# PV as register-addressed TensorE loops in a written order: one decode step over a long KV cache

## The chip, the cores and the metric

One core of one Trainium2 chip. The metric is the device time of one execution in microseconds (us). All executions quoted here were fast (none was over 1.5% above the fastest of the same kernel), and each changed kernel is compared with runs of the kernel before on the same chip. Ratios are the mean time of one kernel's fast runs over that of the other's of the same rounds, so not quite the ratio of the medians that stand beside them.

## The reference

One token through an adaLN-conditioned block: modulation, layer norm, grouped-query attention over a cache of 32768 positions, then a ReLU feed-forward part. All tensors are bf16.

```python
# D = 512, Hq = 32, Hkv = 8 (4 q heads to a kv head), Sk = 32768, Dh = 128, Dff = 1792
sa, ca, ga, sb, cb, gb = split(silu(c) @ w_mod, 6)
h = layernorm(x) * (1 + ca) + sa
q = h @ wq
p = softmax(q @ k_cache.T * Dh ** -0.5)       # per kv head: 4 x 32768
x = x + ga * ((p @ v_cache) @ wo)
h = layernorm(x) * (1 + cb) + sb
out = x + gb * (relu(h @ w1) @ w2)
```

K and V are 134 MB of the 149 MB that the kernel reads.

## The kernel before

The loads run on one queue through a ring of four slots of 4 MB; a load can be issued only when the tile that held its slot has been used for the last time. For each kv head g, a K half is transposed by VectorE and multiplied with a block-diagonal q (`scores`), the softmax follows, and PV (probabilities times V) multiplies 16 columns of the transposed probabilities by V, 64 matmuls a head, accumulated in one bank `o_ps`. While head g's PV runs, head g+1's scores are taken. Cut to what the change and the argument touch:

```python
ring = ctx.enter_context(tc.tile_pool(name="ring", bufs=4))
...
stream = [("wm",), ("wq",)] + [("k", 0, (2 * G, 2 * G + 1)) for G in range(NG)]
for g in range(LAST):
    for G in range(NG):
        stream += [(kind, gg, (2 * G, 2 * G + 1)) for kind, gg in (("k", g + 1), ("v", g))]
stream += [("v", LAST, (0, 1)), ("v", LAST, (2,)), ("wo", 0), ("wo", 1), ("v", LAST, (3,)), ("wo", 2)]
stream += [("w1",)] + [("w2", i) for i in range(len(W2P))]
...
def pv(g, u, js=range(16)):
    ...
    Vsb = need(("v", g, u))
    if g == LAST and u > 1:                       # the narrow form: V as weights
        for j in range(TK):
            nc.tensor.matmul(oT_ps, lhsT=Vsb[:, j, :], rhs=PT_g[:, j % 16, c0:c0 + REP], ...)
        return
    ...
    for j in js:                                  # the wide form
        m = nc.tensor.matmul(
            o_tiles[g][:], lhsT=PT_g[:, j, REP * s0:REP * (s0 + 4)],
            rhs=Vsb.rearrange("p (s j) d -> p s j d", j=16)[:, :, j, :],
            start=(u == 0 and j == 0), stop=(u == end and j == 15))
        pe_order(m)
    if u == end and j == 15:                      # diagonal blocks of o_ps, summed by TensorE
        X = spool.tile([16, 4 * Dh], F32, tag="X", name="X", bufs=1)
        nc.scalar.copy(out=X[:], in_=o_tiles.pop(g)[:])
        for s in range(4):
            nc.tensor.matmul(oT_ps, lhsT=X[:, s * Dh:(s + 1) * Dh], rhs=osel[:, s, :], ...)
...
for g in range(Hkv):                              # order of the program; a scheduler moves within it
    if g + 1 < Hkv:
        build_qbd(g + 1)
    for G in range(NG):
        for u in (2 * G, 2 * G + 1):
            if g + 1 < Hkv:
                scores(g + 1, u)
        if g + 1 < Hkv and G == NG - 1:
            stages = softmax(g + 1)
            pv(g, 2 * G, range(8));  next(stages)
            pv(g, 2 * G, range(8, 16));  next(stages)
            pv(g, 2 * G + 1);  next(stages, None)
            continue
        for u in (2 * G, 2 * G + 1):
            if g == LAST and u == NTILE - 1:
                for i in range(len(WOP) - 1):
                    project(i)
                join_rows()
            pv(g, u)
    normalise(g)
    ...
project(len(WOP) - 1)
```

## Time and profile before

| | before |
|---|---|
| median of 4 runs | 357.38 us (356.87 to 357.7) |
| span of the profiled run | 356.0 us |
| bytes on the load queue | 149.43 MB, 98.0% of the span |
| TensorE, VectorE busy | 81%, 54% |

The prediction below shows the rows that matter most: DMA full to the last slice, K and V landing 29 us after their issue.

This is how TensorE enters the end, from its timeline (start, length, engine, line, operation, output and inputs, count, and the idle time before with what ended it):

```profile
323.59 1.05 PE L468 MATMUL acc_ps<-osel,X 16*128 16x4 f32 x8 [0.35 <-ACT X L466]
324.57 7.07 PE L458 MATMUL o_ps<-Vsb,PT_g 128*16 128x512 bf16 x32
333.35 1.84 PE L448 MATMUL acc_ps<-PT_g,Vsb 128*128 128x4 bf16 x64
```

The last head's PV starts at 324.57 us.

### The profile page before, as it was taken

What the parts mean: (1) busy time and instruction counts of PE and PEld (TensorE: products, weight loads), DVE (VectorE), ACT (ScalarE), POOL (GpSimd) and SP (SyncE); (2) the same over time, 40 slices, a digit from 0 to 9 for tenths busy, and PEclk for the clock granted to TensorE, in tenths of its full rate; (3) what the DMA queues carried; (4) which work ended last, traced back from release to release, by engine and by line L of the source; (5) the groups of instructions that cost most, each with busy time, mean ns of one, the idle gap of its engine ahead of it and who ended that gap; (6) DMA issues with size and microseconds to landing.
All of it is one profiled execution on the core that took longest, in us unless ns stands there. A gap on an engine that the chain in (4) does not pass through costs nothing.

```text
span 356.0 us, 3635 instructions
## 1 busy us (share of the span) xinstructions
PE 287.1 (81%) x1571; PEld 128.5 (36%) x1571; DVE 191.6 (54%) x219; ACT 34.0 (10%) x78; POOL 8.5 (2%) x14
## 2 busy tenths in 40 slices
PE   0466965999699969788896969896978879799874
PEld 0253322444334433334332334333333424244473
DVE  8524697782667366463819373746637290842020
ACT  1023003102100110012000200012000200011020
POOL 9000000000000000000000000000000000000000
PEclk9966789999879998999899969999899969899755
DMA  8999999999999999999999999999999999999993
GB/s 326 437 435 436 423 443 427 422 446 427 429 438 435 420 447 431 423 442 429 431 438 427 433 439 423 438 436 423 435 442 419 442 431 422 442 427 419 390 407 138
DMA packets 6602, 149.66 MB, mean 420 GB/s; under 512 B 697, under 2 KB 698, under 8 KB 1594
## 3 DMA queue, kind: packets, MB, share of 16 engines
q1 hardware_dynamic: 6578, 149.43, 98.0%
q8 instruction: 12, 0.20, 0.2%
q14 instruction: 4, 0.03, 0.0%
q10 hardware_dynamic: 8, 0.00, 0.0%
HBM read 149.42 MB, written 0.00 MB: 420 GB/s over the span
## 4 chain that ended last, share of the span: by engine, by line
DMA 55%; PE 22%; DVE 16%; issue 4%; ACT 1%; SPq 0%; DVEq 0%; ACTq 0%
DMA Ksb<-in_A_k_cache_dram 50%; DVE KTt L375 14%; PE S_ps L384 9%; PE o_ps L458 6%; DMA c_row<-in_c_dram 3%; DMA w_sb<-in_B_w_dram 2%; PE modT_ps L284 1%; PE acc_ps L448 1%; PE q_ps L267 1%; PE mod_ps L267 1%; PE a_ps L510 1%; PE qT_ps L334 1%; PE acc_ps L468 1%; PE acc_ps L530 1%; ACT L243 0%
## 5 line engine op out<-in xcount | busy, mean ns | idle before, releaser
L384 PE MATMUL S_ps<-KTt,qbd 128*128 128x512 bf16 x512 | 135.6, 423 | 39.1 <-DVE KTt L375 39.1
L375 DVE STREAM_TRANSPOSE KTt<-Ksb 128x2048 f32<-128x2048 f32 x64 | 142.5, 2280 | 34.4 <-DMA Ksb<-in_A_k_cache_dram 32.8
L458 PE MATMUL o_ps<-Vsb,PT_g 128*16 128x512 bf16 x480 | 108.4, 379 | 0.0
L384 PEld LDWEIGHTS <-qbd 128*128 128x128 bf16 x512 | 53.4, 105 | 114.8 <-issue 64.4
L458 PEld LDWEIGHTS <-PT_g 128*16 128x16 bf16 x480 | 40.8, 90 | 60.0 <-issue 6.0
L390 DVE TENSOR_SCALAR_CACHE_REDUCE S_g<-S_ps 128x512 f32<-128x512 f32 x16 | 11.1, 692 | 37.7 <-PE S_ps L384 37.7
L355 ACT COPY qbd<-qrep_sb 32x128 bf16<-32x128 bf16 x32 | 9.4, 295 | 161.5 <-PE S_ps L384 160.4
L427 DVE STREAM_TRANSPOSE PT_g<-P_g 128x1024 bf16<-128x1024 bf16 x8 | 9.9, 1238 | 21.7 <-ACT P_g L422 21.7
L482 DVE TENSOR_TENSOR oT_sb<-acc_ps,Linv 128x4 bf16<-128x4 f32 x8 | 1.3, 162 | 25.7 <-PE acc_ps L448 17.2
L468 PE MATMUL acc_ps<-osel,X 16*128 16x4 f32 x64 | 8.4, 250 | 3.2 <-ACT X L466 3.2
L419 ACT ACTIVATE nbias<-Mb_ps 128x1 f32<-128x1 f32 x8 | 1.4, 171 | 89.1 <-PE Mb_ps L417 89.1
L203 PE MATMUL xc_ps<-one,c_bd 8*128 8x1 bf16 x4 | 0.3, 171 | 11.8 <-DVE c_bd L193 11.8
L468 PEld LDWEIGHTS acc_ps<-osel,X 16*128 16x128 f32 x64 | 7.7, 186 | 4.3 <-ACT X L466 4.3
L422 ACT ACTIVATE P_g<-S_g,nbias 128x1024 bf16<-128x1024 f32 x8 | 9.2, 1149 | 0.4 <-ACT nbias L419 0.2
L155 DVE COPY sel<-ident_bf 128x128 bf16<-128x128 bf16 x4 | 7.2, 3544 | 0.0
L466 ACT COPY X<-o_ps 16x512 f32<-16x512 f32 x8 | 4.6, 574 | 22.8 <-PE o_ps L458 22.8
L406 DVE TENSOR_REDUCE Mrow<-mT_ps 1x4 f32<-1x128 f32 x8 | 2.2, 278 | 8.2 <-PE mT_ps L404 8.2
L267 PE MATMUL q_ps<-wq_sb,hT 128*1 128x512 bf16 x32 | 3.6, 627 | 2.6 <-DVE hT L250 2.6
L435 DVE RECIPROCAL Linv<-L_ps 128x4 f32<-128x4 f32 x8 | 1.4, 176 | 7.0 <-PE L_ps L433 7.0
L417 PEld LDWEIGHTS Mb_ps<-ident_f,Mexp 1*128 1x128 f32 x16 | 2.3, 182 | 6.1 <-issue 6.1
L203 PEld LDWEIGHTS <-c_bd 8*128 8x128 bf16 x4 | 0.2, 112 | 11.8 <-DVE c_bd L193 11.8
L284 PE MATMUL modT_ps<-rowsel,mod_rows 128*128 128x4 f32 x16 | 3.9, 375 | 0.5 <-ACT mod_rows L279 0.5
(112 smaller groups left out, 96.6 us busy)
## 6 DMA issues: line engine op xcount, KB each, us to landing
Ksb<-in_A_k_cache_dram SPq DMA_DIRECT2D x16, 4096.0 KB, 29.7
Vsb<-in_A_v_cache_dram SPq DMA_DIRECT2D x15, 4096.0 KB, 28.9
wq_sb<-in_A_wq_dram SPq DMA_DIRECT2D x1, 4096.0 KB, 18.8
Vsb<-in_A_v_cache_dram SPq DMA_DIRECT2D x2, 2048.0 KB, 16.3
wm_sb<-in_w_mod_dram SPq DMA_DIRECT2D x1, 3072.0 KB, 10.3
wo_sb<-in_A_wo_dram SPq DMA_DIRECT2D x1, 2048.0 KB
wo_sb<-in_A_wo_dram SPq DMA_DIRECT2D x2, 1024.0 KB, 9.9
w_sb<-in_B_w_dram SPq DMA_DIRECT2D x1, 1792.0 KB, 9.9
```

The lines of the kernel that those rows point to most:

```text
L155: nc.vector.tensor_copy(out=sel[:, hp, :].rearrange("p (a c) -> p a c", a=4), in_=src)
L267: nc.tensor.matmul(dst[j // 4][32 * (j % 4):32 * (j % 4) + 1, :], lhsT=src_T[:, kt:kt + 1], rhs=w[:, kt, j * 512:(j + 1) * 512], start=(kt ...
L284: nc.tensor.matmul(modT_ps[:, i, ko, :], lhsT=mod_rows[:, i, :].rearrange("q (m ko) -> q ko m", ko=KT)[:, ko, :], rhs=rowsel[:], start=Tru ...
L355: nc.scalar.copy(out=o, in_=i)
L375: nc.vector.transpose(out=KTt[:].bitcast(F32), in_=Ksb[:, 32 * half:32 * half + 32, :].rearrange("p j d -> p (j d)").bitcast(F32),)
L384: nc.tensor.matmul(S_ps, lhsT=qbd[g % 2][:, hp, s, :], rhs=KTv[:, 16 * sl:16 * sl + 16, h, :, par], start=(t4 == 0 and sl == 0 and hp == 0 ...
L390: nc.vector.tensor_scalar(out=S_tiles[g][:, G, :], in0=S_ps, scalar1=1.0, scalar2=None, op0=ALU.mult, op1=ALU.max, accum_out=m_tiles[g][:, ...
L422: nc.scalar.activation(out=P_g[:], in_=S_g[:].rearrange("p g f -> p (g f)"), func=ACT.Exp, bias=nbias[:], scale=scale, accum_out=l_g[:],)
L427: nc.vector.transpose(out=PT_g[:], in_=P_g[:])
L458: m = nc.tensor.matmul(o_tiles[g][:], lhsT=PT_g[:, j, REP * s0:REP * (s0 + 4)], rhs=Vsb.rearrange("p (s j) d -> p s j d", j=16)[:, :, j, : ...
L466: nc.scalar.copy(out=X[:], in_=o_tiles.pop(g)[:])
L468: nc.tensor.matmul(oT_ps, lhsT=X[:, s * Dh:(s + 1) * Dh], rhs=osel[:, s, :], start=(s == 0), stop=(g < LAST and s == 3), skip_group_check= ...
```

## The change

The intent: a shorter TensorE program (PV of six of the eight kv heads as loops over byte offsets), TensorE and VectorE in a written order instead of the scheduler's, the softmax's steps taken between score steps, the masked sum of the four diagonal blocks on VectorE in four steps, and a front with fewer small matmuls. Cut to its core (the front, the renamed tiles and the split of `wo` into 2+4+2 heads, of which the first two parts share a slot, are left out):

```diff
+    LOOPED = Hkv - 2
-    def pv(g, u, js=range(16)):
+    def pv(g, us, js=range(16)):
...
+        if g < LOOPED:
+            with tc.tile_critical():
+                with nc.tensor.Fori(0, 512 - 63, 64) as at:
+                    for b in range(2):
+                        for u, V in zip(us, Vf):
+                            step(u, V, PTf[:, 32 * b + 16 * (u % 2):][:, bass.DynSlice(at, 16)],
+                                 V[:, :, Dh * b:][:, :, bass.DynSlice(at * (Dh // 32), Dh)])
+        else:
+            for u, V in zip(us, Vf):
+                for j in js: ...
-            nc.scalar.copy(out=X[:], in_=o_tiles.pop(g)[:])
-            for s in range(4):
-                nc.tensor.matmul(oT_ps, lhsT=X[:, s * Dh:(s + 1) * Dh], rhs=osel[:, s, :], ...)
+    def blocks(g):
+        nc.vector.tensor_scalar(out=Y[:], in0=o[:, 0], scalar1=smask[:, 0:1], ...)
+        for s in range(1, 4):
+            nc.vector.scalar_tensor_tensor(out=Y[:], in0=o[:, s], scalar=smask[:, s:s + 1], in1=Y[:], ...)
+        if g == LAST:
+            nc.vector.memset(oT_ps, 0.0)
+    def o_cols(g):
+        nc.tensor.matmul(oT_ps, lhsT=Y_tiles.pop(g)[:], rhs=qsel, ...)
+    with tc.manual_schedule(engines={mybir.EngineType.PE, mybir.EngineType.DVE}):
+        ...
+        for g in range(LAST):
+            h = g + 1
+            build_qbd(h)
+            turn_k(h, 0, 0)
+            if soft: next(soft)          # Mrow, Mexp on VectorE: wait for mT on TensorE
+            scores(h, 0, 0)
+            if soft: next(soft)          # Mb, exp
+            open_o(g)                    # VectorE fills o_ps with zeros
+            turn_k(h, 0, 1); scores(h, 0, 1)
+            if g > 0: blocks(g - 1); o_cols(g - 1)
+            turn_k(h, 1, 0); scores(h, 1, 0); turn_k(h, 1, 1); scores(h, 1, 1)
+            ...                          # PT transpose, normalise(g - 1), L, bank_max(h, 0), Linv
+            pv(g, (0, 1))
+            for u in (2, 3): ...         # turn_k, scores
+            bank_max(h, 1)
+            soft = softmax(h)
+            next(soft)                   # m_p
+            if g < LOOPED:
+                pv(g, (2, 3))
+                next(soft)               # mT on TensorE, behind the loop
+                continue
+            next(soft); next(soft)
+            pv(g, (2,), range(6)); ...; pv(g, (2,), range(6, 16)); pv(g, (3,)); ...
+            open_o(LAST); blocks(g); o_cols(g); normalise(g)
+        pv(LAST, (0, 1)); pv(LAST, (2,))
+        blocks(LAST); project(0); o_cols(LAST); project(1); join_rows()
+        pv(LAST, (3,)); normalise(LAST)
+    project(len(WOP) - 1)
```

## The prediction

> **What bounds the kernel now.** I read the page's time slices and queue table first, then the chain that ended last, then the SyncE queue's own waits, then the timeline of one kv head, then the end.
>
> ```profile
> PE   0466965999699969788896969896978879799874
> DMA  8999999999999999999999999999999999999993
> GB/s 326 437 435 436 423 443 427 422 446 427 429 438 435 420 447 431 423 442 429 431 438 427 433 439 423 438 436 423 435 442 419 442 431 422 442 427 419 390 407 138
> q1 hardware_dynamic: 6578, 149.43, 98.0%
> DMA 55%; PE 22%; DVE 16%; issue 4%; ACT 1%; SPq 0%; DVEq 0%; ACTq 0%
> ```
>
> The DMA row is full from the first slice to the last but one. Slices 2 to 36 average 432.5 GB/s, and 149.43 MB at that rate are 345.5 us of the 356.0. The other 10.5 us are the start (slice 1 moves 326 GB/s, some 2.2 us lost), the smaller rows of the last weights (390 and 407 GB/s), and some 5 us after the last bytes. So compute matters only where it lets the queue run dry, or after the last byte. Does it run dry?
>
> ```profile
> SPq L118 <- DVE KTt L375: 134.3, 15, 12.4
> SPq L118 <- PE o_ps L458: 72.3, 8, 9.9
> SPq L118 <- PE L_ps L433: 66.3, 7, 10.5
> Ksb<-in_A_k_cache_dram SPq DMA_DIRECT2D x16, 4096.0 KB, 29.7
> Vsb<-in_A_v_cache_dram SPq DMA_DIRECT2D x15, 4096.0 KB, 28.9
> ```
>
> SyncE waits for ring slots (four of 4 MB), but a 4 MB load lasts 9.7 us at that rate and lands 29 us after its issue: on average two loads are still ahead of it. These waits are slack, not loss.
>
> ```profile
> 129.65 8.88 DVE L375 STREAM_TRANSPOSE KTt<-Ksb 128x2048 f32<-128x2048 f32 x4
> 140.71 7.07 PE L458 MATMUL o_ps<-Vsb,PT_g 128*16 128x512 bf16 x32
> 147.58 8.89 DVE L375 STREAM_TRANSPOSE KTt<-Ksb 128x2048 f32<-128x2048 f32 x4 [6.06 <-DMA Ksb<-in_A_k_cache_dram]
> 152.14 1.90 PE L384 MATMUL S_ps<-KTt,qbd 128*128 128x512 bf16 x8 [0.30 <-DVE KTt L375]
> 350.22 1.02 PE L601 MATMUL ffn_ps<-w_sb,hidT 128*1 128x128 bf16 x32 [1.59 <-DMA w_sb<-in_B_w_dram]
> 351.50 1.02 PE L601 MATMUL ffn_ps<-w_sb,hidT 128*1 128x128 bf16 x24 [0.26 <-DMA w_sb<-in_B_w_dram]
> ```
>
> A head's four loads take 38.7 us (K transposes at 108.85 and again at 147.58 in the full timeline). In them TensorE has four blocks of 32 matmuls at 221 ns (7.07 us), two for scores and two for PV, 28.3 us, and about 1.8 us of small ones: some 8 us of slack per head. VectorE sits idle until a K load lands. The last FFN matmuls wait for the weights' arrival, and from the last arrival (352.10) to the end are 3.9 us. The kernel is bound by its loads.
>
> [...] In this trace 64 pairs of weight load and matmul of the o_T step take 1.84 us, 29 ns a pair[...]. [...] The instruction queue here moved 0.20 MB, 0.2% of the engines' span, so the shorter program (2759 listed TensorE rows become 2072) can save a tenth of a microsecond or so.
>
> **The change, part by part.** Bytes, load order (but for the two first parts of wo, swapped in size) and slots stay. So each part is counted against slack first.
>
> *Front.* Sixteen modT matmuls (3.90 us) become eight fp32 transposes; one such took 0.27 us (the mT row), so 2.2 us. Thirty-two gb matmuls (1.16 us) become one of about 0.5. The q path from 28.85 to 31.94 (copies, 16 matmuls of 2.14 us, a cast) becomes two VectorE transposes of 512 columns (2280 ns for 2048 columns, so about 0.6 us each) and small copies, about 1.7 us. Sum: some 3.5 us earlier, but the first K load lands only at about 30 us[...], so the first transpose moves from 32.4 to about 30. Nothing of this reaches the queue, which then has 10 us and more ahead. Worth 0.
>
> *PV as loops.* Twelve loops of 8 turns with 4 matmuls. Each matmul has one fused register instruction[...] before it, each turn an add and a compare-and-branch. [...] So 8 to 10 us, with 9 as the centre, where it was 7.07.
>
> *A wait that the diff doesn't show.* In the built program the branch into each loop waits for every semaphore at its value in the program so far. One is the K load behind the V that the loop needs, so PV of V(g,01) starts only when K(g+1,23) has landed, 9.7 us later than it might. V's slot comes free later by that much. With K(h,01) landing at 0, V at 9.7, K(h,23) at 19.4: PV loop of the head before 0 to 9, max, scores with softmax and the masked sum between, paced by three transposes in turn behind Mrow, up to 20.4; loop to 29.4, scores and bank maximum to 37.4; next K at 38.7. So a period is 19.4 + 2 x loop, in 38.7: it fits up to a loop of 9.65 us. V's slot is free at 29.4 and its next load must be issued by about 36.7 (the load ahead ends at 38.7): 7 us to spare. The queue stays fed.
>
> *Written order, masked sum.* The X copy (0.57 us on ScalarE) and 8 acc matmuls (1.05 us, 0.7 us of wait in front) become four VectorE sums[...] beside transposes and one matmul: about 1 us less of TensorE per head, in slack.
>
> *End.* PV of V(7,2) is 16 wide matmuls (3.5 us) for 64 narrow ones (1.84), and TensorE comes some 4 us later into the end, held back by the late K wait. But v7(3) is now issued after PV of head 6, not after that of v7(0,1), and w1 after v7(2): one step sooner each. My reckoning leaves the stream 1 to 2 us of slack there. After the last weights the chain is the same: 3.9 us.
>
> Sum: 0 from the front, 0 from the middle, between -0.5 and +1 at the end: **357.5 us**.
>
> **The rivals.** *TensorE becomes the bound.* If a loop costs more than 9.65 us, each head lags by twice the excess; 11 us would be 2.7 us a head, 15 us over five and a half heads, of which some slack is there first: 365 to 370 us. For it: nobody has measured register-addressed matmuls here, and TensorE is already 81% busy. Against: [...]a lag of up to 7 us in V's slots starves nothing. *The late K wait becomes the bound.* With slots freed 9.7 us later, any further stall[...] would let the queue run dry in every head: 360 to 368. For it: the written order makes VectorE's Mrow wait for TensorE's mT behind the loop, and the first half of a head already needs 20.4 of 19.4 us in my sum. Against: the second half gives back 2. *Faster.* If the dips at the end (390 and 407 GB/s) came from late issues, the earlier issues would return up to 2 us: 355.5. Against: in the trace those loads were issued before the stream reached them. Under 350.2 (2% faster) it cannot come: 345.5 us of transfers, 2 at the start and 4 after the last arrival are 351.5.
>
> **Range and chances.** The centre is the bound of the loads, which doesn't move. Up to 1.5 us below it lies the best end; above, half of the two slower rivals. A loop over 10.4 us (over 2% in all) gets 0.17. Range 355.5 to 365; faster 0.02, same 0.80, slower 0.18.
>
> **What would show each step.** The DMA row full to the last slice but one and GB/s near 432 in the middle: bound unchanged. A loop's 32 matmuls in 7 to 9.5 us; over 9.7 with TensorE at 95% and GB/s falling is the first rival. PV's first matmul just after the landing of the next K load, and V's time from issue to landing fallen from 28.9 to about 20 us (K's to 21 to 25): the late wait. First K transpose near 30 us. The last weights landing 3.9 us before the end. The prediction is wrong if the GB/s slices of the middle fall below 425, or if the last weights land over 2 us sooner or later than 352.

The loop's sum (register instructions, weight loads and matmuls, add and branch, the way in and out) came to 8 to 10 us a loop, with 9 as the centre; it is the author's estimate and no more. It enters the forecast as nothing, since 9 is under the 9.65 us that fit: 357.5 us is the time before, 357.38 us, with 0 from the front, 0 from the middle and -0.5 to +1 us at the end. Two smaller terms are cut too: what made up the landing of the first K load at about 30 us, and the length of one of VectorE's four sums (measured later: 293 ns for the first, 339 ns for each of the others).

## More of the kernel before

One more view is needed for the end. These are windows of 4 us; the columns are the length, the busy time of TensorE's matmuls, of its weight loads, of VectorE, ScalarE and GpSimd, then TensorE's granted clock as a share of full speed, the DMA share and GB/s.

```profile
336.00:340.00 4.00, 3.31 (x27) 1.80 (x19) 0.00 (x0) 1.87 (x2) 0.00 (x0) 0.50 0.93 387
340.00:344.00 4.00, 3.23 (x92) 3.08 (x93) 0.56 (x3) 0.00 (x0) 0.00 (x0) 0.50 1.05 448
344.00:348.00 4.00, 3.13 (x86) 2.85 (x84) 1.48 (x11) 0.56 (x2) 0.00 (x0) 0.50 0.95 366
348.00:352.00 4.00, 2.16 (x72) 1.85 (x70) 0.00 (x0) 0.18 (x1) 0.00 (x0) 0.50 0.59 223
```

The loads keep up their rate to about 348 us.

## The result, and the profile after

The changed kernel took 368.98 us (median of 4 runs, 366.08 to 369.79) beside 357.38 us for the kernel before: ratio 1.0311, 95% interval 1.025 to 1.0373. It is slower, and outside the predicted range. The rows of the page after that answer to those of before:

```profile
DMA  8999999999999999999999999999999999996572
GB/s 329 438 428 442 419 439 431 431 442 424 436 428 435 442 424 436 428 431 445 420 442 428 429 442 425 443 419 435 438 428 445 417 436 438 420 426 292 169 286 63
q1 hardware_dynamic: 6592, 149.43, 95.2%
PE 14%; DVE 4%; issue 0%; ACT 0%; DVEq 0%
L490 PE MATMUL o_ps<-Vsb,PT_g 128*16 (+1 forms) x496 | 128.0, 401 | 21.3 <-ACT qbd L387 7.6
Vsb<-in_A_v_cache_dram SPq DMA_DIRECT2D x15, 4096.0 KB, 17.3
```

Slices 2 to 36 average 432.3 GB/s, as before. The middle of the kernel lost nothing. The four last slices hold the whole loss, and the chain that ended last, which was 55% DMA before, now has no DMA in it as far as it could be followed: the end waits for TensorE and VectorE. The windows of the end, as shown for before and with the one ahead:

```profile
332.00:336.00 4.00, 3.29 (x9) 1.42 (x10) 1.01 (x4) 0.00 (x0) 0.00 (x0) 0.55 1.03 434
336.00:340.00 4.00, 4.00 (x12) 1.34 (x11) 0.00 (x0) 0.00 (x0) 0.00 (x0) 0.60 0.36 152
340.00:344.00 4.00, 4.00 (x20) 1.69 (x19) 0.00 (x0) 0.00 (x0) 0.00 (x0) 1.00 0.00 0
344.00:348.00 4.00, 2.68 (x13) 1.00 (x12) 1.18 (x4) 0.00 (x0) 0.00 (x0) 1.00 0.93 305
348.00:352.00 4.00, 2.90 (x26) 0.95 (x25) 0.87 (x4) 0.22 (x1) 0.00 (x0) 0.68 0.84 337
```

The queue runs dry from about 338 to 344 us and then is fed in pieces. TensorE's timeline says why:

```profile
332.71 0.58 PE L528 MATMUL acc_ps<-mask_sb,Y 16*128 16x4 f32 x2 [2.16 <-DVE Y L520]
333.23 13.45 PE L490 MATMUL o_ps<-Vsb,PT_g 128*16 128x512 bf16 x48
348.83 0.60 PE L572 MATMUL a_ps<-wo_sb,o_sb 128*1 128x512 bf16 x8 [2.15 <-DVE a_ps L243]
```

The last head's PV starts at 333.23 us where it was 324.57: 8.66 us later, of which 2.16 are a wait for VectorE's four sums (before, the wait at this place was 0.35 us). Its 48 matmuls take 13.45 us. At the full clock they take 10.53 (experiment e5 has them so). The clock fell to about half behind the wait: the window from 332 to 336 us has 0.55. The kernel before also ran at 0.50 from 336 us on, without such a wait, so the wait is not the only way into the half clock. PV frees the slots: the last part of wo was issued at 343.26 us (before: 335.22), w1 at 346.71 (337.04). Nothing was issued for 13 us before that.

Why is TensorE late? One head of the timeline, all engines but the weight loads, with cuts:

```profile
151.34 8.04 PE L490 MATMUL o_ps<-Vsb,PT_g 128*16 x32 [0.80 <-DVE Linv L471]
159.57 7.10 PE L419 MATMUL S_ps<-KTt,qbd 128*128 128x512 bf16 x32 [0.19 <-PEq L496]
...
166.70 1.22 ACT L387 COPY qbd<-qrep_sb 32x128 bf16<-32x128 bf16 x4 [24.09 <-PE S_ps L419]
...
168.56 8.62 PE L490 MATMUL o_ps<-Vsb,PT_g 128*16 x32 [1.90 <-ACT qbd L387]
...
177.68 0.28 DVE L440 TENSOR_REDUCE Mrow<-mT_ps 1x4 f32<-1x128 f32 x1 [7.87 <-PE mT_ps L437]
```

A loop's 32 matmuls take 8.03 to 8.07 us in five of the six first halves of a head (8.84 in the sixth) and 8.6 to 9.0 us in second halves, where they took 7.07. The second-half loop is entered 1.90 us after the scores. VectorE stands for 7.87 us until TensorE has left that loop, and has three of the four transposes of the next block of scores still to do. From one first-half loop to the first-half loop five heads on, 72.35 to 269.68 us, a head takes 39.47 us; the loads give one each 38.7. So TensorE falls behind a little in each head. Three causes are mixed here (the loop, its entry, the written order) and a fourth stands at the end. The experiments separate them.

### The profile page after: what moved, and what is told of

It is laid out like the page before. It is cut to its first block, busy times and chain, and to the rows that moved or that the text cites. A ratio compares the mean times of both kernels' runs of the same rounds, so it can differ in the third digit from the quotient of the medians.

```text
span 367.9 us, 4059 instructions
## 1 busy us (share of the span) xinstructions
PE 278.1 (76%) x1379; PEld 115.2 (31%) x1379; DVE 205.8 (56%) x266; ACT 28.9 (8%) x70; POOL 8.4 (2%) x14
## 5 line engine op out<-in xcount | busy, mean ns | idle before, releaser
L419 PE MATMUL S_ps<-KTt,qbd 128*128 128x512 bf16 x512 | 121.5, 388 | 30.1 <-DVE KTt L403 28.9
L490 PE MATMUL o_ps<-Vsb,PT_g 128*16 (+1 forms) x496 | 128.0, 401 | 21.3 <-ACT qbd L387 7.6
L419 PEld LDWEIGHTS <-qbd 128*128 128x128 bf16 x512 | 49.9, 98 | 93.8 <-issue 36.7
L490 PEld LDWEIGHTS o_ps<-Vsb,PT_g 128*16 x384 | 34.6, 90 | 85.2 <-issue 60.7
L490 PEld LDWEIGHTS <-PT_g 128*16 128x16 bf16 x112 | 10.4, 95 | 15.6 <-issue 4.1
L518 DVE TENSOR_SCALAR Y<-o_ps,smask 16x128 f32<-16x128 f32 x8 | 2.3, 293 | 13.0 <-PE o_ps L490 13.0
L520 DVE SCALAR_TENSOR_TENSOR Y<-o_ps,smask,Y 16x128 f32<-16x128 f32 x24 | 8.1, 339 | 0.8
L468 PE MATMUL L_ps<-Lexp,ones_f 128*128 128x4 f32 x16 | 2.8, 245 | 4.3 <-DVE Lexp L465 4.3
L528 PE MATMUL acc_ps<-mask_sb,Y 16*128 16x4 f32 x16 | 3.4, 282 | 2.2 <-DVE Y L520 2.2
L468 PEld LDWEIGHTS L_ps<-Lexp,ones_f 128*128 128x128 f32 x16 | 2.9, 203 | 5.6 <-issue 4.8
## 6 DMA issues: line engine op xcount, KB each, us to landing
Ksb<-in_A_k_cache_dram SPq DMA_DIRECT2D x16, 4096.0 KB, 21.7
Vsb<-in_A_v_cache_dram SPq DMA_DIRECT2D x15, 4096.0 KB, 17.3
```

The lines of the kernel that those rows point to most:

```text
L419: nc.tensor.matmul(S_ps_tiles[g], lhsT=qbd[g % 2][:, hp, s, :], rhs=KTv[:, 16 * sl:16 * sl + 16, h, :, par], start=(t4 == 0 and sl == 0 an ...
L468: nc.tensor.matmul(L_ps[:], lhsT=ones_f[:], rhs=Lexp[:], start=True, stop=True)
L490: nc.tensor.matmul(o_tiles[g][:], lhsT=PT, rhs=Vx, start=False, stop=False, skip_group_check=True)
L520: nc.vector.scalar_tensor_tensor(out=Y[:], in0=o[:, s], scalar=smask[:, s:s + 1], in1=Y[:], op0=ALU.mult, op1=ALU.add,)
```

## The experiments

"Period" is the time between the first-half PVs of head 0 and head 5, over five; the loads' own is 38.7. It is lower where a kernel starts its first PV late and then catches up with the loads: so in e1, e8 and, a little, e7, and in the kernel before (37.4). "Last PV" is the start of PV of the last head; e4, e8 and e10 move it ahead of the masked sum. The medians of the kernel before in these rounds, on three chips, were 357.42 to 357.75 us.

| | change to the changed kernel | median us | ratio to before (95%) | period us | last PV us |
|---|---|---|---|---|---|
| (changed) | | 368.98 | 1.0311 (1.0250–1.0373) | 39.47 | 333.23 |
| e1 | PV written out | 359.80 | 1.0072 (1.0012–1.0132) | 36.8 | 324.88 |
| e2 | written out, in the critical section | 362.28 | 1.0159 (1.0117–1.0200) | 38.77 | 328.04 |
| e3 | loops in three heads only | 358.87 | 1.0054 (1.0001–1.0107) | – | 324.74 |
| e4 | last PV ahead of the masked sum | 364.26 | 1.0201 (1.0174–1.0227) | 39.36 | 331.05 |
| e5 | maximum after the loop in the program | 368.92 | 1.0325 (1.0306–1.0345) | 39.33 | 333.43 |
| e6 | eight matmuls a turn | 362.13 | 1.0124 (1.0099–1.0150) | 38.69 | 328.14 |
| e7 | one K transpose moved up on VectorE | 362.23 | 1.0118 (1.0094–1.0142) | 38.28 | 327.78 |
| e8 | e1 and a reordered end | 356.91 | 0.9977 (0.9964–0.9990) | 37.0 | 322.42 |
| e9 | e5, ScalarE in written order too | 366.16 | 1.0245 (1.0207–1.0284) | 39.09 | 332.04 |
| e10 | e6 and e8's end | 357.03 | 0.9986 (0.9970–1.0003) | 38.89 | 325.79 |
| e11 | before, with the new front alone | 356.98 | 0.9986 (0.9969–1.0003) | – | 323.24 |
| e12 | e9, maximum behind a K transpose | 363.78 | 1.0156 (1.0126–1.0185) | 38.73 | 330.20 |

All were correct against the reference. The first four were to separate the loops, their entry, a lag from a lasting cost, and the end.

### e1: PV written out

```diff
-        if g < LOOPED:
+        if g < 0:
```

> The changed kernel with its PV loops written out again (32 matmuls a half head, no loop, no branch), all else and the whole written order kept. Theory A (the loops put TensorE behind the loads: a head with loops has a period of some 39.3 us in the trace of the changed kernel where the loads give 38.7, so TensorE came 7.3 us later into the end): TensorE enters the end with the V of the last head some 5 to 7 us sooner, the queue runs dry for less than 4 us, and the time is 359 to 363 us. Theory B (the written order is the cause: the softmax between score steps makes the block of scores 11.3 us where it was 8.8, and the sum on VectorE comes before the last PV): the loops go and the time stays at 366 to 369 us. Theory C (the end alone: the 2.2 us wait ahead of the last head's PV and the half clock after it): 366 to 369 us too, with the queue dry as before.

Measured: 359.80 us, last PV at 324.88 us, within 0.3 us of the kernel before. Theory A holds: by the medians 9.2 of the 11.6 us belong to the loops, in the place in which they stand, and the other 2.4 us are not the loops' doing. e1's four runs spread from 357.31 to 361.57 us, so the split is good to some 2 us only; the times of the last PV are the sharper evidence. In e1's trace TensorE waits at the same two places in the end:

```profile
324.37 0.58 PE L528 MATMUL acc_ps<-mask_sb,Y 16*128 16x4 f32 x2 [2.16 <-DVE Y L520]
338.89 0.60 PE L572 MATMUL a_ps<-wo_sb,o_sb 128*1 128x512 bf16 x8 [2.15 <-DVE a_ps L243]
349.81 1.63 PE L691 MATMUL hidT_ps<-h2T,w_sb 128*128 128x1 bf16 x56 [0.66 <-DVE h2T L275]
```

The last line shows that the feed-forward part no longer waits for weights; TensorE and VectorE set the end.

### e2: the critical section without the loop

```diff
             with tc.tile_critical():
-                with nc.tensor.Fori(0, 512 - 63, 64) as at:
-                    ...
+                for j in range(16):
+                    for u, V in zip(us, Vf):
+                        c0 = 32 * j + 16 * (u % 2)
+                        step(u, V, PTf[:, c0:c0 + 16], V[:, :, Dh * j:Dh * (j + 1)])
```

> As e1, but the written-out 32 matmuls stand inside the critical section that the loops stood in, so the entry still waits for every semaphore, and only the loop itself is gone. If the loop's own cost is what counts (8.0 to 8.8 us for 32 against 7.1): the same time as e1 within 1 us, 359 to 363 us. If the entry's waits (0.8 us ahead of a first half, 1.9 us ahead of a second half, in the trace of the changed kernel) are what counts: 365 to 369 us, the same as the changed kernel.

Measured: 362.28 us, 2.5 us over e1 and 6.7 under the changed kernel: not within 1 us of e1, and clear of the second expectation. By the medians the section's entry accounts for some 2.5 of the 9.2 us and the loop itself for the rest, with this order around it. With e1's spread the 2.5 is not sharp, but the last PV, 3.2 us later than in e1, agrees. TensorE's waits in e2 name what the entry costs once TensorE keeps up (columns: us in total, times, longest):

```profile
PE o_ps L490 <- DMA Ksb<-in_A_k_cache_dram: 15.6, 5, 5.0
```

PV waits for K, which it doesn't read. The changed kernel has no such line: after head 0, TensorE is so far behind there that K has landed before it is asked for.

### e3: loops in the first three heads only

```diff
-        if g < LOOPED:
+        if g < 3:
```

> Loops in the first three heads alone, the other heads written out. If the lag builds up by some 0.7 us a head with loops and is worked off by heads without (their period on TensorE is some 36 us, 2.5 us under that of the loads): nothing is left of it at the end, and the time equals that of e1 within 0.7 us. If each loop costs time for good (3 of 6 heads): halfway between e1 and the changed kernel, 364 to 366 us.

Measured: 358.87 us, the last PV at 324.74 us, both as e1 (359.80, 324.88). Six loops early in the kernel cost nothing that shows. The loss is no sum over loops; it is the lag with which TensorE reaches the end, and heads without loops work it off.

### e4: the last PV ahead of the masked sum

```diff
             open_o(LAST)
+            pv(LAST, (0, 1))
             blocks(g)
             o_cols(g)
             normalise(g)
-        pv(LAST, (0, 1))
```

> The changed kernel with all its loops; the last head's first PV half stands in TensorE's order ahead of the masked sum of the head before, so it needs not wait for VectorE's four steps. If the end's written order and the half clock that follows the wait are the cause (theory C): the wait of 2.2 us goes and the clock stays up, 3 to 5 us less, 364 to 366 us; if the lag into the end is all of it, 367.5 to 369 us.

Measured: 364.26 us, 4.7 under the changed kernel with every loop kept. The last PV starts 2.2 us sooner, and its 48 matmuls run at full clock (7.07 and 3.62 us). So the wait and the half clock behind it are real parts of the loss.

These four leave a question: is the loop itself too slow, or does anything that shortens a head by 0.7 us do as well? The next runs each take about 1 to 2 us off a head in a different way.

### e5 and e9: two tries at the entry that did not reach it

```diff
+            if g < LOOPED:
+                pv(g, (2, 3))
             bank_max(h, 1)
             soft = softmax(h)
             next(soft)
             if g < LOOPED:
-                pv(g, (2, 3))
                 next(soft)
                 continue
```

> The changed kernel with its loops; only the second-half loop of each head stands in the program ahead of VectorE's copy of the scores with their maximum and of the maximum's reduction, so its entry no longer waits for these (they end 0.9 us after the scores in the trace of the changed kernel). Theory P (a period of TensorE of 39.3 to 39.4 us a head, just over the 38.7 us of the loads, is what puts it behind; anything that takes about 1 us from the period takes the whole of the growing lag): period near 38.4, the lag into the end 3 to 5 us smaller, 363 to 366 us. If the wait on ScalarE's build of the block-diagonal q stays behind it, only 0.6 us a head: 365 to 367 us. If the entry's wait doesn't matter: 368 to 370 us.

Measured: 368.92 us, a miss. Entry stayed at 1.90 us. e9 adds ScalarE to the engines in written order:

```diff
-    with tc.manual_schedule(engines={mybir.EngineType.PE, mybir.EngineType.DVE}):
+    with tc.manual_schedule(engines={mybir.EngineType.PE, mybir.EngineType.DVE, mybir.EngineType.Activation}):
```

> e5 moved nothing: the second-half loops were still entered 1.90 us after the scores, and the wait named was ScalarE's build of the block-diagonal q, which starts when the scores of the head end and takes 1.22 us, and which the scheduler had moved ahead of the loop. Here ScalarE too runs in the written order (where the build comes after the loop), on top of e5's swap. If that wait with VectorE's is what holds the entry: 1.90 falls to about 0.9 us, the period of 39.4 us by some 1.0 us to 38.4 us, under the loads', so the lag no longer grows: TensorE enters the last head's PV some 4 to 5 us sooner and the time is 362 to 366 us. If the entry stays at 1.9 us, or something else takes the place of the wait: 368 to 370 us.

Measured: 366.16 us, between the two expectations, and with an interval that overlaps the changed kernel's. The entry fell only to about 1.8 us; where a wait is named (two of the six) it is VectorE's maximum. The built programs explain it: the branch into the loop waits for each engine's semaphore at the value that the scheduler has reached by then, and in both kernels VectorE's value is the same as in the changed kernel (96 at head 1's second loop; in e12 below it is 94). Moving a line in the program did not move the wait. Neither run tells whether the entry matters. e5's profile is useful for another thing, the windows of its end:

```profile
332.00:336.00 4.00, 2.88 (x14) 1.38 (x15) 1.38 (x5) 0.00 (x0) 0.00 (x0) 1.00 0.99 410
336.00:340.00 4.00, 4.00 (x20) 1.71 (x19) 0.00 (x0) 0.00 (x0) 0.00 (x0) 1.00 0.40 172
```

Here the clock stayed at 1.00 after the same wait, the last PV took 10.53 us, and the span was 364.1 us; in the changed kernel's profile, with the last PV starting within 0.2 us of the same time, it was 367.9. So the fall of the clock costs some 3 to 4 us here (2.9 in the PV itself), and it came in some of the profiled executions only. With that wait of 2.15 to 2.16 us ahead of the last PV, its 48 matmuls took 11.86 to 13.45 us in six of nine profiles (the changed kernel, e1, e2, e3, e7, e12) and 10.53 us in the other three (e5, e6, e9); in e4, e8 and e10, which have no such wait there, 16 of them took 3.62 us. A clock that falls in some executions only fits the spread of the changed kernel's runs (366.08 to 369.79 us) and of e1's (357.31 to 361.57), though the clock of unprofiled runs at that place is not recorded, so the spread's cause is not shown.

### e12: the entry reached

This edit is against e9, cut: a guard, left out here, skips the transpose where it stood.

```diff
                 pv(g, (2, 3))
+                turn_k(h + 1, 0, 0)
             bank_max(h, 1)
```

> In e5 and e9 the entry of the second-half loops still waited for VectorE's maximum: the built program showed that the two waits at the entry have the same values on VectorE as in the changed kernel, since the scheduler had VectorE pass the loop's branch after the maximum all the same, so these two took away ScalarE's part alone, 0.12 us of 1.90. Here the next head's first K transpose stands between, and the built program shows VectorE's branch ahead of the maximum and the wait two instructions lower. If the entry's wait then ends: 1.8 falls to about 0.9 us, the period from 39.1 (e9) to some 38.3 us, under the 38.7 of the loads, TensorE enters the last head's PV near 328 us as in e6 and e7 (e9: 332.0 us), and the time is 361 to 364 us. If the entry itself costs that much (drain and branch): still 1.7 us or more and 365 to 367 us.

Measured: 363.78 us, as the first expectation had it. Two of the second-half loops:

```profile
207.40 8.72 PE L490 MATMUL o_ps<-Vsb,PT_g 128*16 x32 [0.77 <-issue]
284.34 8.63 PE L490 MATMUL o_ps<-Vsb,PT_g 128*16 x32 [1.03 <-DMA Ksb<-in_A_k_cache_dram]
```

The entry fell to between 0.77 and 1.03 us in four of the six, the period to 38.73 us, the loads' own. TensorE reached the last PV at 330.20 us, not at the 328 expected: the slow loops still put it 2 us behind e6.

### e6: eight matmuls a turn

```diff
-                with nc.tensor.Fori(0, 512 - 63, 64) as at:
-                    for b in range(2):
+                with nc.tensor.Fori(0, 512 - 127, 128) as at:
+                    for b in range(4):
```

> The changed kernel with eight matmuls in a turn and four turns a loop instead of four and eight. A turn of four matmuls took 1.00 us in first halves and 1.09 us in second halves against 0.884 us written out. If the turn's add and branch are the cost, 32 matmuls take 0.5 us (first half) and 0.8 us (second half) less, the period falls by 1.3 us to some 38.1 us, under the loads', and the time is 362 to 366 us. If the register work of every matmul is the cost: the same mean of a matmul as in the changed kernel within 5 ns, and 368 to 370 us.

Measured: 362.13 us. The gain came as expected, but the loop's cost was not halved; it vanished:

```profile
207.29 7.07 PE L490 MATMUL o_ps<-Vsb,PT_g 128*16 x32 [1.94 <-ACT qbd L387]
128.59 8.75 PE L490 MATMUL o_ps<-Vsb,PT_g 128*16 x32 [3.48 <-DMA Ksb<-in_A_k_cache_dram]
```

The first line is 32 matmuls in 7.07 us, as long as written out. The second is what comes with it: now that TensorE keeps up with the loads, some loops wait for the K load, here 3.48 us, and this one then took 8.75 us; the page's slice from 126.1 to 135.1 us has a granted clock of 0.8, the slices on either side 0.9. The instructions of the loops in the changed kernel's trace suggest why eight help (durations least, median, most in ns):

```profile
L490 PEldq FUSED_REGOPS  x288: 74/74/74, 72.4 to 294.8; - x144
L497 PEldq ALU_OP  x96: 32/34/39, 72.8 to 294.9; - x96
L497 PEldq COMPARE_BRANCH  x96: 76/208/230, 72.9 to 295.0; - x96
```

A turn of four spends 4 x 74 (the first of them 78) + 34 + 208 = 542 ns on these, of the 1.00 us it lasts in a first half; so the four weight loads and four matmuls take some 57 ns each of the sequencer (an estimate, from the difference). With eight matmuls this gives, again as an estimate, 0.84 + 16 x 0.057 = 1.75 us, just under the 1.77 us of array time (8 x 221 ns): the same costs, which would then be hidden. Why a turn is slower in second halves (1.08 to 1.13 us) is not settled; their loops have one more add of 36 ns a turn.

### e7: one K transpose moved up

```diff
             turn_k(h, 0, 0)
+            turn_k(h, 0, 1)
             if soft:
...
             open_o(g)
-            turn_k(h, 0, 1)
```

> The changed kernel with its loops; only the second K transpose of a head is moved up in VectorE's written order, ahead of the softmax step that waits for TensorE to leave the second-half loop. In the trace of the changed kernel VectorE stands idle some 7.9 us behind that loop, and the 32 score matmuls after it then take 11.3 us because VectorE has all its work still to do. Theory P with the written order as a full cause of the period (rather than the loops alone): the block falls from 11.3 to about 9 us, the period to some 37.1 us, nothing of the lag is left, and the time is 360 to 364 us although every loop is still there. If the loops alone are the cause: 367 to 370 us.

Measured: 362.23 us, with every slow loop still in place. From the second-half loop to the next first-half loop a head took 19.8 us (mean of five) where the changed kernel took 21.9. VectorE now has one more transpose done before it waits for the loop:

```profile
177.57 0.28 DVE L440 TENSOR_REDUCE Mrow<-mT_ps 1x4 f32<-1x128 f32 x1 [5.86 <-PE mT_ps L437]
182.27 1.89 PE L419 MATMUL S_ps<-KTt,qbd 128*128 128x512 bf16 x8 [0.70 <-DVE KTt L403]
```

So the loops alone are not the cause, and neither is the written order, which e1 kept: the lag needs both. Taking away the cost of the turn (e6) or this order (e7) brings the period down to the loads', and the time to the same 362 us.

### e8 and e10: the two together, with the end mended

e8 is e1 with this end (e10 the same on e6, loops kept). Cut: the start and stop flags, and the old zero fill of `a_ps` in `project`, which goes:

```diff
-        if g == LAST and us[0] == NTILE - 1:
+        if g == LAST and us[0] >= NTILE - 2:      # V tile 2 of the last head narrow again
...
-        if g == LAST:
-            nc.vector.memset(oT_ps, 0.0)
...
+            open_o(LAST)
+            a_rows.append(row_bank("a_ps"))        # both zero fills ahead of PV
             pv(g, (2,), range(6, 16))
             pv(g, (3,))
             next(soft)
             next(soft, None)
-            open_o(LAST)
             blocks(g)
+            pv(LAST, (0, 1), range(8))
             o_cols(g)
             normalise(g)
-        pv(LAST, (0, 1))
+            nc.vector.memset(oT_ps, 0.0)
+        pv(LAST, (0, 1), range(8, 16))
         pv(LAST, (2,))
```

> The PV written out (as e1), and the end reordered: the zero fills of the last head's sums moved ahead of PV, the masked sum of head 6 taken between the halves of the last head's first PV, and the third V tile of the last head multiplied the narrow way (64 matmuls with V as weights, 1.84 us in the kernel before, against 3.5 us wide). If the 2.4 us by which e1 is behind the kernel before lie in the order and form of the end alone: TensorE's chain ends some 4 us sooner than in e1, the loads (last weights landed at about 350.4 us in e1, 351 us in the kernel before) set the end again, and the time is 355.5 to 357.5 us, 0 to 0.5% below the kernel before. If the end doesn't count: 359 to 361 us as e1.

> The loops kept, with eight matmuls a turn (e6, in which most loops took 7.07 us, as long as written out) and the reordered end of e8. Its loops still wait at their entry for K loads: in e6 three of the twelve waited 3.5 to 3.8 us[...], and TensorE came to the last head's PV 3.2 us later than in e1. If e8's end leaves at least 3 us of slack there: 356.7 to 357.5 us, as e8. If the late K wait shows through: 358.5 to 360.5 us.

Measured: 356.91 us and 357.03 us. The end of e8 waits for weights again:

```profile
347.42 1.65 PE L691 MATMUL hidT_ps<-h2T,w_sb 128*128 128x1 bf16 x56 [0.77 <-DMA w_sb<-in_B_w_dram]
349.89 1.02 PE L703 MATMUL ffn_ps<-w_sb,hidT 128*1 128x128 bf16 x32 [0.82 <-DMA w_sb<-in_B_w_dram]
```

e8 is faster than the kernel before by 0.2% (interval 0.1 to 0.4%), the best of this study, though far under the 2% at which the record calls a kernel faster. e10 shows that the loops can be had for nothing, though they gain nothing either: its interval includes the kernel before. What a shorter program could save was small from the start: the instruction queue of the changed kernel moved 0.15 MB where it had moved 0.20, and 0.05 MB at the measured 432 GB/s are 0.1 us (an estimate from these two). The three waits of e8's end (sum, zero fill, wide PV) were mended together, so their single shares in its gain are open.

### e11: the front alone, on the kernel before

Its edit is the front's part of the change (x and c rows in one tile, transposes for the modT matmuls, one matmul for the gb rows, VectorE transposes for q) put into the kernel before, with all else as it was.

> The kernel before with the front of the change alone (the x and c rows in one tile, the transposes and the short row matmuls), its own schedule, PV and masked sum kept. The prediction said that the front's some 2 us sooner stay hidden behind the loads: 0 effect, 357.0 to 357.8 us, ratio 0.998 to 1.002. If the loads start or end sooner with it: 355.5 to 356.8 us.

Measured: 356.98 us, ratio 0.9986 with an interval from 0.9969 to 1.0003. The front is hidden; at most 0.3% could be in it.

## Why the prediction was wrong, point by point

1. *The bound, and the middle.* Right. The loads ran at 432.3 GB/s in slices 2 to 36, and the lag in V's slots starved nothing there (V's landing fell to 17.3 us after issue, expected about 20; K's to 21.7, expected 21 to 25).
2. *The front.* Right. First K transpose at 30.42 us (expected about 30), behind a wait of 1.67 us for the K load; the one gb matmul took 0.46 us (expected about 0.5), and e11 shows no effect.
3. *The loop.* The estimate, 8 to 10 us with the way in and out, was near for the body: 8.04 and 8.6 to 9.0 us. Of its terms the runs show a fused register instruction of 74 ns and an add and compare-and-branch of 242 ns together. The way in measured 0.74 to 1.53 us and the way out 0.19 in first halves, and mostly 1.90 in and 0.19 to 0.35 out in second halves, since the wait for every semaphore includes VectorE's maximum and ScalarE's build of the next q, of which the prediction had seen only the K load. e12 shows that taking most of this part away is enough for a head to fit.
4. *"So a period is 19.4 + 2 x loop, in 38.7: it fits up to a loop of 9.65 us."* **This step failed.** The loop-to-loop working gave 20.4 us from a second-half loop to the next first-half loop and 17 from there to the next: 37.4, with 1.3 to spare. The trace has 21.9 and 17.6: 39.5. Of the 2.1 us that are missing, 1.5 are in the first term, with its second-half loop (a body of 8.83 us on average), and 0.6 in the second term, with its long entry. In the first term VectorE, idle behind the loop, is what paces the block of scores, with the bank's zero fill (0.48 us) and the four sums (1.38 us) put between the transposes; the prediction had counted these as "beside transposes". e7 takes 2.1 us from this one term and gets 6.8 us back. The margin of 1.3 us was smaller than the error of the sum.
5. *The masked sum.* Right about TensorE (0.42 us a head in place of 1.05: 3.4 us of L528 over eight heads), wrong about where it counts: the sums lie on VectorE's path in the first half of each head, and on TensorE's at the end.
6. *"My reckoning leaves the stream 1 to 2 us of slack there."* **This step failed too, and by the most microseconds.** TensorE came to the last PV 8.66 us later, not "some 4 us". Behind that came three things not in the reckoning at all: the wait of 2.16 us for the sums (part of the 8.66), the half clock after it (10.53 us becoming 13.45), and 2.15 us behind the last head's sums and the zero fill of `a_ps`. w1 was issued 9.7 us later than before, and the queue ran dry. e4 takes 4.7 us back in this place, e8 shows that with PV written out and a mended end nothing is lost.
7. *The rivals.* The first, TensorE becoming the bound (365 to 370 us), is what happened, by its mechanism, though not by the loop alone. With in and out a loop took some 10.4 us on average (8.5 + 1.6 + 0.2), over the limit of 9.65; a part of the 1.6 is the bank maximum, which the 19.4 had counted already. The second is real too, but only where TensorE keeps up: e2, e6 and e7 wait for K, and reach the last PV some 3 us later than e1. In the changed kernel it is hidden behind the first.

The parts do not add up to the 11.6 us as a sum. Taking the turn's cost (e6), the order (e7) or most of the entry's wait (e12) away each brings the period to the loads' and returns 5 to 7 us, and taking all that the loops cost away (e1) returns 9.2, not the sum. This fits a threshold: once a head is no longer than its loads, a further saving has no lag left to remove.

## What to carry to other kernels

Where a kernel is bound by its loads, compare each engine's period per stage with the period of the loads, add up every wait on that period, and treat a margin of a few per cent as none: a stage that is 0.7 us too long (here 39.47 us a head against 38.7) shows nothing while the buffers absorb it (three heads with loops in e3: 358.87 us, e1 without: 359.80), and the whole lag is paid at the end, where no loads are left to hide behind. Written orders need the same care at the seams as in the steady part: an engine that waits for a loop on another should have its independent work ahead of that wait (one K transpose moved ahead of it in e7: 362.23 us in place of 368.98). And a loop on TensorE wants enough matmuls in a turn: here 32 of them took 8.03 to 9.01 us with four in a turn, and with eight 7.07 or 7.08 us, as long as written out, in nine of twelve loops (e6).
